# Linear attention and a gated feed-forward on one core: last stores on SyncE, batch 2's loads held by batch 1's q, and a new written order

## Chip, core and metric

The kernel runs on one core of a Trainium2 chip. The metric is the device time of the program in microseconds (us), lower is better. The core's engines are named as the profile names them: PE (TensorE; PEld is its weight load), DVE (VectorE), ACT (ScalarE), POOL (GpSimd), SP (SyncE). SP, ACT and POOL issue DMAs; the rows SPq, ACTq and POOLq are their sequencers.

## What is computed

Inputs q, k, v are 8 batches x 8 heads x 576 positions x 64, in float32. The attention is linear, with the feature map phi, and its output, laid out as 4608 tokens x 512, goes through a product of two projections and two more matrices:

```python
phi(x) = where(x > 0, x, exp(x) - 1) + 1
kv  = einsum('bhsd,bhse->bhde', phi(k), v);  z = sum(phi(k), axis=2)
num = einsum('bhsd,bhde->bhse', phi(q), kv)
den = einsum('bhsd,bhd->bhs', phi(q), z)[..., None] + 1e-06
x   = (num / den), heads side by side          # 4608 x 512
out = (((x @ w1) * (x @ w2)) @ w3) @ w_out     # w1, w2: 512 x 1024; w3: 1024 x 1024; w_out: 1024 x 512
```

## The kernel before

**Tiling.** 576 positions are 4 x 128 and 64 left over. For each batch the first 512 are one chunk (0 to 7). The 64 left of two batches are put together as a "pair" on 128 partitions; the four pairs make chunk 8. All matmuls are in bfloat16, with sums in float32. Since nothing stands between w3 and w_out, the kernel first multiplies them into one 1024 x 512 matrix (`wf_sb`).

**Steps.** Each piece of work is a small function registered under a short name (`@step`, lines 92 to 449), and the whole program is a list of such steps with arguments, the string `ORDER` (line 451 on). Each engine does its own instructions strictly in that order; semaphores between the engines are set where data or buffers require them. Nothing else decides the order, so "a new order" means a new string. The steps that matter here, with b for the batch, c for the chunk, p for the pair:

- `const:i`: memsets; `const:1` makes the 128 x 128 identity on POOL. `warm:n,i`: n matmuls on zeros, whose result nobody reads. `zr` clears half of a pair's phi(k) tile.
- Loads: `ld:k,b,h0,nh,queue` (L119) loads heads of k, q or v of a batch, 1 MB for 8 heads; `lr` (L127) the left-over 64 positions of one batch, `lp` (L135) those of a pair in two DMAs, 128 KB each; `l3` (L159) a row block of w3, `lo` (L151) of w_out, `lw` (L144) columns of w1 or w2. The last letter is the issuing queue: g POOL, s SP, a ACT. Full loads share 5 buffers (`ld`, with w3's rows among them).
- phi: `x` (exp on ACT, L166), `t` (max and add on DVE, L172), `m` (min on DVE, L180); `xr`, `tr`, `mr` the same for a pair. `v` and `vr` (L217, L225) cast v to bfloat16; a last letter a or v here means ACT or DVE.
- Attention: `kv:b,hp` (L238, L241) is phi(k)^T v with z for two heads, into PSUM; `kc` and `kh` (L248, L259) copy it out; `qt` and `qc` (L267, L273) transpose phi(q) on PE for batches 0 and 1, `qd` and `qdr` (L279, L285) by a DMA transpose on SP for the others; `na` (L291) multiplies, `nd` (L297 to L299) divides on DVE, three instructions; `nar`, `ndr` for pairs. `xp` and `xc` (L333, L338) transpose x on PE for batches 0 to 2, `xd` and `xdr` (L343, L348) on SP.
- Weights: `w3t`, `w3c` transpose w3's rows on PE and copy them; `wa`, `wf` (L373, L381) form the product w3 w_out, and `wc` copies it.
- Feed-forward: `f:c,f` (L393) is one 128-column block of x w1 and x w2 (8 matmuls of 512 columns), `fk` a part of one; `ac` (L407) copies the first on ACT and `ab` (L412) multiplies on DVE. `o:c,m` (L418) is the last product for 128 tokens (8 matmuls), `oc` (L424) its copy to SBUF and `st` (L436) its store: one DMA of 256 KB, for chunk 8 two of 128 KB. `ol:7,3` (L445 to L449) is o, oc and st of one unit in two column halves: the first is copied by DVE and stored by SP, the second by ACT both.

PSUM has four single banks for `f`, `o`, `xp`, `w3t` and warm, and two double ones for `kv`, `na` and `wa`.

**Gates.** `GATES` (line 523) names steps that must wait for another one's DMA to land although no data ties them. Before, they are two: `ld:q,2` waits for `ld:q,1`, and `lr:k,1` for `lw:0,0`. A held DMA holds all that stands behind it on its queue.

**Order around the change.** POOL makes the identity, then issues w3's and w_out's rows, batch 0, the rest of the weights and batch 1, and after that all stores but ol's. SP issues the left-over loads and all loads from batch 2 on, in the order `lr:k,1 lr:v,1 lp:v,1 ld:v,2 lp:k,1 ld:k,2 ld:q,2 ld:v,3 ...`, and the transposes between them. Batch b + 1's attention is woven between the f and o units of chunk b. At the end PE does `f:8,1 ol:7,3 o:6,0 o:6,3 f:8,2 f:8,4 o:6,2 o:8,3 o:8,1 o:8,0 o:8,2 o:7,0`.

Of the kernel before, what the change touches and what calls it, by code (L numbers as in the profile page):

```python
# [9 lines left out]
BF16 = mybir.dt.bfloat16  # L10
# [3 lines left out]
P = 128  # L14
# [4 lines left out]
def kernel(  # L19
# [12 lines left out]
    B, H, S, D = q.shape  # L32
# [51 lines left out]
    def got(d, key, pool, shape, dtype, tag, name=None):  # L84
        if key not in d:
            d[key] = pool.tile(shape, dtype, tag=tag, name=name or tag)
        return d[key]
# [114 lines left out]

    @step
    def zr(p, w):
        d = ph["kr", p, w] = phr_p.tile([P, H * D], BF16, tag="kr", name="kr")
        nc.vector.memset(d[rows_of(1 - w)], 0.0)

    @step
# [240 lines left out]
                queue.dma_start(out=dst[:, cols], in_=d[r, cols])  # L449
# [12 lines left out]
    ld:k,1,0,8,g kh:0,3,1,a kh:0,3,0,a na:0,1 na:0,0 qc:0,2,2,a w3t:6 nd:0,1 ld:q,1,0,8,g w3t:7 w3c:6,a
    nd:0,0 na:0,3 xp:0,1 w3c:7,a nd:0,3 ld:v,1,0,4,g lr:k,1,s na:0,2 xp:0,0 wf:6 lr:v,1,s nd:0,2
    xc:0,1,a xc:0,0,a ld:v,1,4,4,g fk:0,0,0,2 wc:6,v xp:0,2 xp:0,3 xc:0,2,a xc:0,3,v fk:0,0,2,1
    fk:0,0,3,1 ac:0,0,a ab:0,0 f:0,2 ac:0,2,a f:0,3 xr:k,0,1 tr:k,0,1 ab:0,2 ac:0,3,a mr:k,0,1 wf:7
    ab:0,3 f:0,5 wc:7,a vr:1,v ac:0,5,a f:0,7 ab:0,5 x:k,1,0,4 t:k,1,0,4 t:k,1,4,4 f:0,6 ac:0,7,a
    m:k,1,0,1 x:k,1,4,4 ab:0,7 m:k,1,0,0 ac:0,6,a m:k,1,4,2 f:0,4 m:k,1,4,3 x:q,1,4,4 lp:v,1,s t:q,1,0,4
    ab:0,6 ac:0,4,a ld:v,2,0,8,s f:0,1 x:q,1,0,4 t:q,1,4,4 ab:0,4 v:1,0,4,a m:q,1,0,1 m:q,1,4,2
    v:1,6,2,a m:q,1,4,3 kv:1,0 m:q,1,0,0 kv:1,1 ac:0,1,a lp:k,1,s kv:1,3 v:1,4,2,v kc:1,0,1,1,a qt:1,2,2
    kc:1,0,1,0,v kh:1,3,1,a kh:1,3,0,v ab:0,1 qt:1,0,2 qc:1,2,2,a kv:1,2 qc:1,0,2,v o:0,0 kh:1,2,0,a  # L470
    ld:k,2,0,8,s kh:1,2,1,a na:1,2 oc:0,0,a na:1,0 o:0,2 nd:1,2 st:0,0,g ld:q,2,0,8,s v:2,4,4,a vr:2,v
    nd:1,0 vr:3,a xp:1,2 na:1,1 oc:0,2,v v:2,0,4,a xp:1,0 na:1,3 nd:1,1 o:0,1 st:0,2,g xc:1,0,a
    ld:v,3,0,8,s nd:1,3 xc:1,2,a xp:1,1 oc:0,1,v xp:1,3 o:0,3 xc:1,1,a tr:k,1,2 st:0,1,g xr:k,1,2
# [24 lines left out]
    ac:4,1,a f:4,2 ld:v,7,0,8,s ab:4,1 ac:4,2,a f:4,5 ab:4,2 x:q,6,4,4 t:q,6,4,4 t:q,6,0,4 x:q,6,0,4
    f:3,1 m:q,6,4,2 m:q,6,4,3 ac:4,5,a m:q,6,0,0 m:q,6,0,1 ac:3,1,a ab:4,5 o:4,0 qd:6 x:k,6,4,4 ab:3,1
    t:k,6,0,4 x:k,6,0,4 o:4,3 t:k,6,4,4 oc:4,0,a tr:q,0,2 xr:q,0,2 m:k,6,4,2 st:4,0,g m:k,6,4,3  # L500
    ld:k,7,0,8,s m:k,6,0,1 kv:6,2 oc:4,3,v o:4,2 mr:q,0,2 st:4,3,g m:k,6,0,0 kv:6,0 oc:4,2,v kv:6,1
    qdr:0 kv:6,3 v:7,0,4,a o:4,1 st:4,2,g kc:6,0,2,1,v v:7,4,4,v kc:6,0,2,0,v na:5,1 oc:4,1,v f:3,5
    nd:5,1 st:4,1,g ac:3,5,a xd:5 na:6,0 na:6,3 ab:3,5 o:3,1 nd:6,3 nd:6,0 o:3,3 oc:3,1,v x:k,7,0,4
    t:k,7,4,4 st:3,1,g ld:q,7,0,8,s x:k,7,4,4 t:k,7,0,4 o:3,0 m:k,7,0,1 oc:3,3,a m:k,7,0,0 m:k,7,4,2
    st:3,3,g m:k,7,4,3 kv:7,0 oc:3,0,a kv:7,2 kv:7,3 st:3,0,g kv:7,1 o:3,2 kc:7,0,2,1,v kc:7,0,2,0,v
    na:6,2 oc:3,2,v na:6,1 f:5,7 nd:6,1 st:3,2,g nd:6,2 ac:5,7,a f:5,6 xd:6 ab:5,7 ac:5,6,a nar:0 nar:1
    ab:5,6 f:5,3 x:q,7,4,4 t:q,7,4,4 lp:q,1,s x:q,7,0,4 ndr:1 f:5,2 m:q,7,4,3 ac:5,3,a m:q,7,4,2 ab:5,3
    ac:5,2,a t:q,7,0,4 f:5,4 m:q,7,0,0 ab:5,2 ac:5,4,a m:q,7,0,1 ndr:0 qd:7 f:6,1 ab:5,4 ac:6,1,a f:6,7
    xdr:0 ab:6,1 ac:6,7,a lp:q,2,s f:6,4 ab:6,7 lp:q,3,s ac:6,4,a f:6,2 ab:6,4 ac:6,2,a na:7,3 na:7,2
    ab:6,2 f:6,6 nd:7,2 xr:q,1,2 tr:q,1,2 ac:6,6,a mr:q,1,2 f:6,5 nd:7,3 qdr:1 ab:6,6 ac:6,5,a na:7,0  # L510
    f:5,1 ab:6,5 nd:7,0 ac:5,1,a f:6,0 ab:5,1 ac:6,0,a f:5,0 ab:6,0 xr:q,2,2 tr:q,2,2 ac:5,0,a mr:q,2,2
    na:7,1 qdr:2 f:5,5 ab:5,0 xr:q,3,2 tr:q,3,2 nd:7,1 ac:5,5,a nar:2 mr:q,3,2 xd:7 nar:3 ab:5,5 o:5,1
    ndr:2 ndr:3 o:5,0 qdr:3 oc:5,1,a st:5,1,g xdr:1 o:5,2 oc:5,0,a st:5,0,g o:5,3 oc:5,2,a st:5,2,g
    f:7,0 oc:5,3,a st:5,3,g ac:7,0,a nar:4 f:7,6 ab:7,0 ndr:4 ac:7,6,a nar:5 f:7,3 ab:7,6 ndr:5 ac:7,3,a
    xdr:2 nar:7 f:7,1 ab:7,3 ac:7,1,a ndr:7 f:7,4 ab:7,1 ac:7,4,a f:7,7 ab:7,4 ac:7,7,a nar:6 f:7,5
    ab:7,7 ndr:6 ac:7,5,a xdr:3 f:7,2 ab:7,5 ac:7,2,a f:6,3 ab:7,2 ac:6,3,a o:7,1 ab:6,3 o:7,2 oc:7,1,a
    st:7,1,g o:6,1 oc:7,2,a st:7,2,g f:8,5 oc:6,1,a st:6,1,g ac:8,5,a f:8,0 ab:8,5 ac:8,0,a f:8,3 ab:8,0
    ac:8,3,a f:8,6 ab:8,3 ac:8,6,a f:8,7 ab:8,6 ac:8,7,a f:8,1 ab:8,7 ac:8,1,a ol:7,3 ab:8,1 o:6,0 o:6,3
    oc:6,0,a st:6,0,g f:8,2 oc:6,3,a st:6,3,g ac:8,2,a f:8,4 ab:8,2 ac:8,4,a o:6,2 ab:8,4 o:8,3 oc:6,2,v
    st:6,2,g o:8,1 oc:8,3,a st:8,3,g o:8,0 oc:8,1,a st:8,1,g o:8,2 oc:8,0,v st:8,0,g o:7,0 oc:8,2,v  # L520
    st:8,2,g oc:7,0,a st:7,0,g
    """
    GATES = "ld:q,2,0,8,s<ld:q,1,0,8,g lr:k,1,s<lw:0,0,256"
    ctx.enter_context(tc.manual_schedule())
    gates = dict(g.split("<") for g in GATES.split())

# [36 lines left out]
```

## Time and profile before

| | |
|---|---|
| median of 3 runs | 253.93 us (253.4 to 255.26) |
| profiled execution, its own time | 255.21 us |
| its span, first to last instruction | 253.5 us |
| mean granted PE clock | 0.987 |
| bytes moved | 50.06 MB, mean 198 GB/s |
| PE / DVE / ACT / POOL busy | 237.5 / 163.9 / 122.4 / 43.9 us |

A profile is one execution. Times in it count from the span's start. In a timeline row the first number is the start, the second the duration, then engine, line, operation, output<-inputs, shape and count; in square brackets stands how long the engine sat idle before it, and who ended that. In the chain of waits a row is a piece of the path that ended last; "issue" is time for which no wait is shown. The view of stretches gives for each the busy time and count of PE, PEld, DVE, ACT and POOL, then the granted clock, the DMA engines' share and GB/s. Ends of matmuls are modelled; starts are measured. Of a DMA the row on its queue is the issue alone; the landing is told separately.

### The profile page before, as it was taken

The numbers are of one execution on the slowest core, as the hardware profiler recorded it, in microseconds if no ns is written. First come the engines' busy times: TensorE is split into PE (matmuls) and PEld (weight loads), VectorE is DVE, ScalarE is ACT, GpSimd is POOL, SyncE is SP. The second block draws the span as 40 slices with busy tenths as digits, with TensorE's granted clock in tenths as the row PEclk, the third lists the DMA queues.
The fourth block names the chain that finished last, engine by engine and source line by source line (L and its number), as shares of the span: only waits on it lengthen the run. The fifth ranks groups of instructions, "written<-read, shape, count | busy, mean of one in ns | idle before, by whom it ended". The sixth has DMA issues, their size and how long they took to land.

```text
span 253.5 us, 4049 instructions
## 1 busy us (share of the span) xinstructions
PE 237.5 (94%) x1482; PEld 126.1 (50%) x1498; DVE 163.9 (65%) x364; ACT 122.4 (48%) x190; POOL 43.9 (17%) x74
## 2 busy tenths in 40 slices
PE   4997889979999999999999999999999999999991
PEld 4843854445544554554544454544544544445440
DVE  7407774877878999959557989786873564141320
ACT  3408554876857774666654814263442323322210
POOL 8544820001100210021000022100002000200133
PEclk9799999999999999999999999999999999999997
DMA  6999999999999998999999599866319311301154
GB/s 116 199 266 349 212 198 306 299 231 307 318 252 254 319 281 228 242 247 324 212 275 348 133 287 203 304 127 125 82 21 188 106 21 21 127 0 51 73 124 124
DMA packets 68915, 50.06 MB, mean 198 GB/s; under 512 B 41312, under 2 KB 64096, under 8 KB 68896
## 3 DMA queue, kind: packets, MB, share of 16 engines
q1 hardware_dynamic: 58768, 28.97, 49.0%
q0 software_dynamic: 9984, 20.71, 31.4%
q8 instruction: 11, 0.18, 0.3%
q10 hardware_dynamic: 144, 0.13, 0.2%
q14 instruction: 8, 0.07, 0.1%
HBM read 38.80 MB, written 9.44 MB: 190 GB/s over the span
## 4 chain that ended last, share of the span: by engine, by line
PE 69%; DMA 19%; DVE 5%; issue 2%; POOL 2%; ACT 1%; POOLq 0%; ACTq 0%
PE b_ps L393 22%; PE a_ps L393 22%; PE o_ps L418 19%; DMA v<-in_v_dram 8%; DMA q<-in_q_dram 5%; DMA w_sb<-in_moe_w_dram 4%; DMA wo<-in_moe_w_out_dram 3%; PE kvp L238 2%; DVE xn L299 2%; PE nd L291 2%; POOL w3b L159 1%; PE ndr L316 1%; POOL out_dram L436 1%; PE o_ps L445 1%; DVE r L298 1%
## 5 line engine op out<-in xcount | busy, mean ns | idle before, releaser
L393 PEld LDWEIGHTS <-w_sb 128*128 128x128 bf16 x576 | 55.5, 98 | 63.9 <-issue 0.6
L412 DVE TENSOR_TENSOR ab<-a_sb,b_ps 128x512 bf16<-128x512 f32 x72 | 48.9, 684 | 44.1 <-PE b_ps L393 40.8
L407 ACT COPY a_sb<-a_ps 128x512 f32<-128x512 f32 x72 | 42.0, 584 | 60.4 <-PE a_ps L393 55.7
L393 PE MATMUL a_ps<-xt,w_sb 128*128 128x512 bf16 x256 | 66.0, 379 | 0.4 <-ACT xt L338 0.4
L393 PE MATMUL b_ps<-xt,w_sb 128*128 128x512 bf16 x256 | 66.0, 379 | 0.0
L418 PE MATMUL o_ps<-wf_sb,ab 128*128 128x512 bf16 x267 | 62.7, 379 | 0.7 <-DVE ab L412 0.2
L436 POOL DMA_DIRECT2D out_dram<-o_sb x39 | 22.1, 567 | 193.5 <-ACT o_sb L424 167.8
L418 PEld LDWEIGHTS <-ab 128*128 128x128 bf16 x280 | 26.6, 98 | 29.0 <-DVE ab L412 0.3
L424 ACT COPY o_sb<-o_ps 128x512 f32<-128x512 f32 x24 | 14.0, 584 | 33.7 <-PE o_ps L418 31.3
L299 DVE TENSOR_TENSOR xn<-nd,r 128x512 bf16<-128x512 f32 x32 | 22.1, 691 | 1.1
L166 ACT ACTIVATE e<-q 128x1024 bf16<-128x1024 f32 x16 | 16.5, 1056 | 1.0 <-DMA q<-in_q_dram 1.0
L166 ACT ACTIVATE e<-k 128x1024 bf16<-128x1024 f32 x16 | 16.4, 1058 | 0.5 <-DMA k<-in_k_dram 0.5
L238 PE MATMUL kvp<-vt,k 128*128 128x130 bf16 x128 | 11.2, 220 | 2.0 <-ACT vt L217 1.2
L217 ACT CAST vt<-v 128x1024 bf16<-128x1024 f32 (+1 forms) x11 | 10.2, 934 | 5.6 <-PE kvp L238 3.1
L424 DVE COPY o_sb<-o_ps 128x512 f32<-128x512 f32 x11 | 7.6, 686 | 8.1 <-PE o_ps L418 8.0
L180 DVE TENSOR_TENSOR k<-t,e 128x512 bf16<-128x512 bf16 x32 | 12.2, 419 | 0.6 <-ACT e L166 0.3
L180 DVE TENSOR_TENSOR q<-t,e 128x512 bf16<-128x512 bf16 x32 | 11.9, 419 | 0.2
L238 PEld LDWEIGHTS <-k 128*128 128x128 bf16 x128 | 9.0, 97 | 5.8 <-issue 2.7
L291 PE MATMUL nd<-kvb,qt 128*128 128x130 bf16 x128 | 10.9, 220 | 1.0 <-DVE kvb L248 0.4
L172 DVE TENSOR_SCALAR t<-k 128x1024 bf16<-128x1024 f32 x16 | 10.5, 686 | 1.2 <-DMA k<-in_k_dram 1.2
L172 DVE TENSOR_SCALAR t<-q 128x1024 bf16<-128x1024 f32 x16 | 10.9, 687 | 0.4 <-DMA q<-in_q_dram 0.4
L291 PEld LDWEIGHTS <-qt 128*128 128x128 bf16 x128 | 8.7, 97 | 4.9 <-DVE xn L299 1.0
(70 smaller groups left out, 196.1 us busy)
## 6 DMA issues: line engine op xcount, KB each, us to landing
out_dram<-o_sb POOLq DMA_DIRECT2D x31, 256.0 KB, 5.4
v<-in_v_dram SPq DMA_DIRECT2D x6, 1024.0 KB, 11.9
k<-in_k_dram SPq DMA_DIRECT2D x6, 1024.0 KB, 9.0
q<-in_q_dram SPq DMA_DIRECT2D x6, 1024.0 KB, 8.9
w3b<-in_moe_w_dram POOLq DMA_DIRECT2D x8, 256.0 KB, 8.2
v<-in_v_dram POOLq DMA_DIRECT2D x3, 512.0 KB, 19.1
k32r<-in_k_dram SPq DMA_DIRECT2D x8, 128.0 KB, 10.8
v32r<-in_v_dram SPq DMA_DIRECT2D x8, 128.0 KB, 5.0
```

Of the source, the lines that this page charges most:

```text
L166: return nc.scalar.activation(out=e[:, 0:nh * W], in_=raw[n, b][:, h0 * W:(h0 + nh) * W], func=AF.Exp)
L172: nc.vector.tensor_scalar(out=d[:, 0:nh * W], in0=raw[n, b][:, h0 * W:(h0 + nh) * W], scalar1=0.0, scalar2=1.0, op0=ALU.max, op1=ALU.add)
L180: nc.vector.tensor_tensor(out=d[:, hp].rearrange("p j u d -> p u j d"), in0=ts[n, b, h0][:, s].rearrange("p (u j d) -> p u j d", u=2, j=NJ ...
L238: nc.tensor.matmul(dst, kj[:, hp, j].rearrange("p u d -> p (u d)"), vt[:, j, 2 * hp:2 * hp + 2, :].rearrange("p h e -> p (h e)"), start=(j ...
L291: nc.tensor.matmul(o[:, j // 2, (j % 2) * 256:(j % 2) * 256 + PW], sb["qt", b][:, hp, j * P:(j + 1) * P], kvb[b][:, hp].rearrange("p u e - ...
L299: nc.vector.tensor_tensor(out=dst, in0=o[:, :, :, 0:D], in1=r.unsqueeze(3).to_broadcast(list(r.shape) + [D]), op=ALU.mult)
L393: nc.tensor.matmul(o, w[:, kc, f * P:(f + 1) * P], xt_of(c)[:, :, kc, :], start=(kc == 0), stop=(kc == KC - 1))
L407: return copy_of[eng](out=d, in_=ps["a", c, f])
L412: nc.vector.tensor_mul(out=d[:, f, :], in0=sb["a", c, f], in1=ps["b", c, f])
L418: nc.tensor.matmul(d, sb["ab", c][:, f, m * P:(m + 1) * P], wf_sb[:, f, :], start=(f == 0), stop=(f == FC - 1))
L424: return copy_of[eng](out=d, in_=ps["o", c, m])
L436: queue_of[queue].dma_start(out=dst, in_=sb["o", c, m][r])
```

## The change

No function computes anything else than before, and the steps are the same but for queues and engines. What differs:

- `zr` takes its tile by `got`, so that `zr:0,0` may now stand after `mr:k,0,0` in the order.
- Two gates become six: `lp:k,1`, `ld:k,2`, `lp:v,1`, `ld:q,2` and `ld:v,2`, all of batch 2's transfers, wait for `ld:q,1` to land; `lr:k,1` waits as before.
- Stores of chunk 8 and of units 7,1, 7,2 and 7,0 are issued by SP instead of POOL; `ol:7,3` is PE's last unit.
- The order is another one throughout. SP's loads come as k, q, v of a batch, instead of v first; `const:1` follows `l3:4`; `w3t:5 w3t:4` stand before `wa:7`; `wf:7` before the first `fk`; some copies change between ACT and DVE.

```diff
     def zr(p, w):
-        d = ph["kr", p, w] = phr_p.tile([P, H * D], BF16, tag="kr", name="kr")
+        d = got(ph, ("kr", p, w), phr_p, [P, H * D], BF16, "kr")
         nc.vector.memset(d[rows_of(1 - w)], 0.0)
...
-    GATES = "ld:q,2,0,8,s<ld:q,1,0,8,g lr:k,1,s<lw:0,0,256"
+    GATES = "lp:k,1,s<ld:q,1,0,8,g ld:k,2,0,8,s<ld:q,1,0,8,g lp:v,1,s<ld:q,1,0,8,g ld:q,2,0,8,s<ld:q,1,0,8,g ld:v,2,0,8,s<ld:q,1,0,8,g lr:k,1,s<lw:0,0,256"
```

The new order in the stretches that the prediction speaks of (start; PE from the last wa to the first fk; batch 1; the transpose xd:3; the end):

```
const:0 const:2 lr:k,0,s const:9 l3:0 lr:v,0,s const:11 l3:1 warm:26,0 const:3 l3:2 l3:3 lo:0,2
xr:k,0,0 const:6 lo:2,2 const:8 const:7 lo:4,2 zr:0,1 tr:k,0,0 lo:6,2 mr:k,0,0 const:10 l3:4 const:4
const:1 l3:5 zr:0,0 const:5 w3t:0 ld:k,0,0,4,g warm:8,1 w3c:0,a w3t:1 ...
... wa:6,1 l3:6 w3t:5 w3t:4 w3c:5,a wa:7,1 l3:7 t:k,0,0,4 w3c:4,a wf:5 ...
... wf:7 nd:0,3 xc:0,1,v nd:0,2 xp:0,3 fk:0,0,0,2 wc:7,v xc:0,3,a xp:0,2 xc:0,2,v fk:0,0,2,1 fk:0,0,3,1
...
ac:0,5,a f:0,4 ab:0,5 ac:0,4,a t:k,1,0,4 x:k,1,4,4 f:0,6 t:k,1,4,4 x:k,1,0,4 ab:0,4 m:k,1,4,2
ac:0,6,a f:0,7 m:k,1,0,0 m:k,1,0,1 ab:0,6 x:q,1,0,4 lp:k,1,s t:q,1,0,4 f:0,3 ac:0,7,a m:q,1,0,0
ld:k,2,0,8,s m:q,1,0,1 v:1,0,4,a m:k,1,4,3 ab:0,7 ac:0,3,a kv:1,1 t:q,1,4,4 qt:1,0,2 x:q,1,4,4
ab:0,3 kv:1,0 o:0,2 v:1,6,2,a kc:1,0,1,1,v lp:v,1,s m:q,1,4,3 qc:1,0,2,a m:q,1,4,2 kc:1,0,1,0,a
v:1,4,2,a qt:1,2,2 oc:0,2,v na:1,1 ld:q,2,0,8,s kv:1,2 qc:1,2,2,a st:0,2,g nd:1,1 kv:1,3 o:0,3
kh:1,2,1,a kh:1,3,0,a kh:1,3,1,v kh:1,2,0,v ld:v,2,0,8,s xp:1,1 x:k,2,0,4 t:k,2,4,4 na:1,2 na:1,0
oc:0,3,v o:0,1 xr:k,1,2 nd:1,2 st:0,3,g x:k,2,4,4 ld:k,3,0,8,s nd:1,0 xc:1,1,a na:1,3 xp:1,2
oc:0,1,a m:k,2,4,3 o:0,0 nd:1,3 xc:1,2,a st:0,1,g tr:k,1,2 vr:3,a t:k,2,0,4 xp:1,3 vr:2,a xp:1,0
m:k,2,0,0 x:q,2,0,4 xc:1,3,v lp:k,2,s xc:1,0,v m:k,2,0,1 oc:0,0,a f:1,1 ...
...
v:4,4,4,a qd:4 na:3,2 f:2,2 ab:2,6 v:4,0,4,a nd:3,2 ac:2,2,a nd:3,0 f:2,1 ab:2,2 x:k,5,0,4 t:k,5,0,4
ac:2,1,a kv:4,1 t:k,5,4,4 kv:4,2 lp:v,3,s x:k,5,4,4 kv:4,0 ab:2,1 na:3,3 kv:4,3 nd:3,3 o:2,1
kc:4,0,2,1,a kc:4,0,2,0,a qdr:0 m:k,5,0,1 m:k,5,4,2 m:k,5,0,0 o:2,2 m:k,5,4,3 xr:k,3,2 xd:3 oc:2,1,v
tr:k,3,2 st:2,1,g mr:k,3,2 na:4,2 oc:2,2,v o:2,0 nd:4,2 st:2,2,g na:4,0 oc:2,0,v o:2,3 nd:4,0
st:2,0,g vr:6,a ld:q,5,0,8,s na:4,1 oc:2,3,v na:4,3 nd:4,3 st:2,3,g f:3,7 ...
...
f:8,1 ab:8,2 ac:8,1,a f:8,0 ab:8,1 ac:8,0,a f:8,4 ab:8,0 ac:8,4,a f:8,7 ab:8,4 ac:8,7,a o:6,1 ab:8,7
o:8,2 oc:6,1,a st:6,1,g o:8,3 oc:8,2,a st:8,2,s o:8,0 oc:8,3,v st:8,3,s f:7,1 oc:8,0,a st:8,0,s
ac:7,1,a o:8,1 ab:7,1 o:7,1 oc:8,1,v st:8,1,s o:7,2 oc:7,1,v st:7,1,s o:7,0 oc:7,2,a st:7,2,s ol:7,3
oc:7,0,v st:7,0,s
```

## The prediction

> **What bounds the kernel now.** I read the page first: busy times and the slices.
>
> ```profile
> span 253.5 us, 4049 instructions
> PE 237.5 (94%) x1482; PEld 126.1 (50%) x1498; DVE 163.9 (65%) x364; ACT 122.4 (48%) x190; POOL 43.9 (17%) x74
> ...
> DMA  6999999999999998999999599866319311301154
> ```
>
> PE is the bound, but "busy" takes in pipelined waiting. Start to start, a 512-column matmul takes 0.216 us in this trace; counting every matmul of the program so (a unit f or o 8 x 0.216 = 1.73, kv 0.28, na or xp 0.22, qt 0.44) gives 231.5 us, the same before and after, since the same units are only reordered. The last matmul ends at 247.8: about 16 us of PE's time is waiting, and 5.7 us follow it. The DMA row says that transfers run without a pause for the first 145 us. The windows table places the waiting:
>
> ```profile
> 38.00:51.50 13.50, 13.50 (x64) 6.14 (x63) 9.00 (x18) 9.08 (x14) 0.00 (x0) 1.00 1.10 294
> 51.50:65.60 14.10, 11.91 (x102) 7.19 (x102) 10.66 (x28) 9.97 (x18) 1.65 (x3) 1.00 1.13 291
> 65.60:150.00 84.40, 83.85 (x515) 43.33 (x518) 69.59 (x156) 52.38 (x79) 7.06 (x12) 1.00 1.02 260
> 150.00:228.60 78.60, 78.35 (x424) 38.05 (x427) 47.80 (x106) 28.79 (x47) 6.97 (x12) 1.00 0.49 117
> ```
>
> The second column is the stretch, the third PE's busy time. After 65.6 only 0.8 us is idle in 163 us. So there are three places: the start (to 38), batch 1's attention (51.5 to 65.6), and the end. PE's own timeline, and the chain of waits, for batch 1:
>
> ```profile
> 52.92 0.22 PE L241 MATMUL kvp<-vrz,kr 128*128 128x130 bf16 x1
> 54.34 0.39 PE L238 MATMUL kvp<-vt,k 128*128 128x130 bf16 x4 [1.20 <-ACT vt L217]
> ```
>
> ```profile
> 33.15 20.48 DMA v<-in_v_dram
> 53.63 0.02 issue
> 53.65 0.64 ACT vt L217
> ```
>
> Batch 1's v lands at 53.6, 20.5 us after its issue. The DMA view of 31.5 to 53.6 says who shared the engines with it:
>
> ```profile
> q0 software_dynamic: 2768, 4.63, 86.8%
> q1 hardware_dynamic: 2708, 1.13, 29.2%
> ```
>
> q1 is SP's queue: 1.13 MB, of which only 0.26 (two lr loads) is batch 1's. 0.87 MB is ld:v,2 (issued 35.7) and the pair loads of batches 2 and 3. The end, from the chain, and the two halves of unit ol from the timeline:
>
> ```profile
> 244.39 0.70 DVE o_sb L424
> 245.09 1.70 issue
> 246.79 0.46 POOL out_dram L436
> 247.25 0.07 issue
> 247.31 0.88 POOL out_dram L436 x2
> 248.20 0.15 issue
> 248.35 0.53 POOL out_dram L436
> 248.88 0.56 POOLq L558
> ```
>
> ```profile
> 230.16 0.38 SPq L449 DMA_DIRECT2D out_dram<-o_sb  x1
> ...
> 230.98 0.37 ACTq L449 DMA_DIRECT2D out_dram<-o_sb  x1
> ```
>
> PE is done at 247.8 and the last copy at 248.4, but POOL still issues stores until 249.4, five in a row at 0.53 each, after 1.7 us in which the profile shows nothing that it waited for.
>
> **What the Trainium skill says.** "DMA: Bandwidth & Descriptors", section "Issuing engines are not separate DMA queues": transfers from SP, ACT and POOL run on the same 16 engines and interleave. The trace agrees (the two queues above). So holding SP's loads leaves the engines to POOL's. The same page, "Latency and other measured facts", gives about 0.6 us to the first byte for SP's path and 1 us for POOL's; here a 128 KB store lands 2.0 us after its issue on SP and 2.5 on POOL, the same direction. "TensorE: Matmul & The Clock Gate", Part 1: after some 3.4 us of idleness PE runs at half clock, 107 ns for 128 columns against 56. The trace shows both (8 transposes 1.06 us at 9.4, 0.61 at 11.15).
>
> **The change part by part.**
>
> *Start.* POOL's first l3 starts at 0.74 where the identity's two instructions stand now, instead of 1.45: 0.7 earlier. POOL's issues are chained to landings (from the ninth on, each starts just after the landing of the one eight before), so I carry 0.6 of it to all POOL loads. The identity moves behind l3:4, ends near 7.0 by POOL's row durations, and w3t:0 goes from 6.2 to 7.0; its warm-up risk is up to 1 us. Placing w3t:4 and 5 before wa:7 removes most of the 1.7 us wait for w3t; wf:7 (1.73) moves ahead of the first f into waiting time. PE would reach batch 1's kv about 2.3 us earlier, 49.5 for 51.8. None of that is kept unless v is there.
>
> *Gates.* lp:k,1, ld:k,2, lp:v,1, ld:q,2 and ld:v,2 wait for batch 1's q: 30.7 + 18.2 = 48.9 now (the DMA issues), so 48.3. SP holds nothing else between. Until 48 the hardware queue took little besides lr, so q gains nothing but the 0.6. Then v: the software queue has 0.55 MB left at 48, which at about 310 GB/s is 1.8 us; v's halves land near 49.6 and 50.4, not 51.2 and 53.6. The second is 3.2 earlier.
>
> *Batch 1's attention.* First half's cast on ACT (1.05) behind x:q,1,0,4 and ac:0,7: done near 51.1; kv:1,1 at 51.2 for 52.4 now. ACT then has ac 0.58, x 1.06, v 0.63, qc 1.0, kc 0.26, v 0.63: 55.3, so kv:1,2 at 55.4. PE fills with o:0,2 and qt, then o:0,3 to 57.7. DVE: nd:1,1 to 56.4, two kh, t:k,2 0.69, oc 0.69, nd:1,2 and nd:1,0 (1.1 each) to 60.8, nd:1,3 to 62.1, tr, t, two xc (0.42 each): 64.1. So f:1,1 starts at 64.1, the first f of chunk 1 now at 65.7: **1.6 us gained**, DVE's chain keeping the rest. Bounds: nothing (v no earlier), 3.2 (all of v's gain).
>
> *What is late next.* Batch 2's k, issued after lp:k,1 at about 49.6, lands near 55 for 62.7 now, wanted at 56.8. q2 lands about 59, v2 62.5 (now 58.4), wanted at 64 and 67.5. By 53.6 the engines have moved the same bytes, in another order. From there k3 to k5 are wanted earlier: by PE work placed before them, 58.5 for 71.8, 74.2 for 88.7, 90.3 for 97.2; v later. Counted as the tenth load, k5 moves 6.9 us. Loads arrive barely in time now (q3 lands at 76.5, its first reader starts at 76.6). With SP's order I get k4 at 85 (wanted 87), v4 98 (99.6), k5 102 (103.3). No stall, 1 to 2 us of slack.
>
> *Transposes on SP.* xd:3 now has 12 us to f:3,7, in the new order 6.5 (four o, four na and a kv, less the wait for nd:3,3), behind qdr:0; they take 4.3 to 7.5 from issue to landing: 0 to 1 us lost, taken as zero against the 0.8 idle us after 65.6 that an order may recover. xd:7 has 7.9, transfers being thin there. Copies swapped between ACT and DVE (0.58 against 0.69) are hidden by f units there: zero; if cover were gone, 0.1 each.
>
> *End.* Stores of chunk 8 and three of chunk 7 move to SP, 7 more DMA steps (11 DMAs at 0.38, far under the 1.73 of an o). ol moves to the end at the same PE work. From ol now: PE ends 230.54, ACT's half is issued 230.98 and lands 1.9 later, 2.4 after PE. DVE copies its half to 230.13 and then oc:7,0 (0.69) to 230.85; st:7,0, 256 KB, lands about 2.3 after its issue: 2.7 after PE's end. Now it is 252.1 - 247.8 = 4.3 (last issue 248.9 plus 3.3, the longest landing among the last ten). **1.6 us gained**; bounds 1.0 and 2.2. The 1.4 us after the last landing stay.
>
> Sum: 253.5 - 1.6 - 1.6 = 250.3 for the span. The profiled execution took 255.2 (span and 1.7 around it), above the median of 253.93; applied to the median: **250.7**.
>
> **Rivals.**
> 1. *Only the end* (chance 0.20): v is ahead, but ACT and DVE, 10 and 10.7 us busy of 14.1 there, set f:1 as now. For it: their chain above already keeps half. Against: the 1.2 us wait is v's. 253.9 - 1.6 = 252.3.
> 2. *All is kept* (0.17): the full 3.2 of v, 1.6 at the end, 0.8 of later idle time and 0.4 of landing: 247.9.
> 3. *Loads become the bound* (0.18, the slow side): the hardware queue starts 0.87 MB behind and doesn't recover it, so that k5 lands where it does now (108.2) instead of at 103.3; DVE's t:k,5 stands ahead of ab:2,1 and nd:3,3, and PE waits for both. That is 4.9 us lost, 255.6; with 0.87 MB at 260 GB/s, 3.3 more: 258.9. It ends my gain when k5 lands after 106.5 and is over 1% slower after 109. Against: the same bytes by 53.6, and a gap in demand (k5 to q5) after it.
> That the gates do nothing is no rival: SP's loads issued 32.8 to 48.5 are all named.
>
> **How the numbers follow.** Forecast 0.45 (249.4 to 252.0), rivals 0.20, 0.17, 0.18. 1% is 2.5 us, about what a measurement of this kernel can tell from no change: faster below 251.4. Most of the forecast and rival 2 give 0.56; the rest of the forecast, rival 1 and a third of rival 3 are the same, 0.32; slower 0.12. Range 247.8 to 255.0, which leaves the outer part of rival 3 and a little of 2.
>
> **What would show it.** Right: v's second half lands near 50.4, kv:1 starts near 51.2, the first f of chunk 1 near 64, the last landing 2.7 after PE's end. Wrong: DVE or ACT waiting for k or q of batches 2 to 5 with PE idle behind them; f:3,7 waiting for xd:3; PE in f later than 65.7; a half-clock stretch past 12 us.

## The result and the profile after

The change moved nothing that can be measured. With 20 runs of each side by side, the kernel before took 255.03 us (253.4 to 257.91) and the changed one 255.3 us (254.17 to 256.29); the ratio is 1.0009, 95% interval 0.999 to 1.0028. The prediction was 250.7. Of the 4.6 us between, 1.1 are the first median of before, 253.93 from three runs, which more runs put at 255.03; 3.2 are the gain that was forecast and didn't come, and 0.3 lie between the two medians.

The profiled execution of the changed kernel took 255.47 us. Its page has the same span as before within 0.2 us. PE is 0.8 us busier, but 16 of its 1498 matmuls are missing from the trace of before (x1482 there), so that this difference says little:

```profile
span 253.3 us, 4047 instructions
PE 238.3 (94%) x1498; PEld 126.7 (50%) x1498; DVE 165.0 (65%) x364; ACT 125.2 (49%) x190; POOL 37.4 (15%) x63
...
DMA  6999999999999999999993999999406413000543
```

The view of stretches, with the same four stretches (stretch, its length, then PE, PEld, DVE, ACT and POOL busy):

```profile
38.00:51.50 13.50, 12.98 (x67) 6.05 (x66) 9.86 (x21) 7.15 (x11) 0.00 (x0) 1.00 1.06 297
51.50:65.60 14.10, 13.33 (x112) 7.76 (x109) 13.21 (x33) 13.00 (x22) 1.65 (x3) 1.00 1.13 295
65.60:150.00 84.40, 82.71 (x520) 43.09 (x521) 69.88 (x160) 54.40 (x81) 6.34 (x12) 1.00 1.05 255
150.00:228.60 78.60, 78.43 (x420) 37.82 (x419) 45.53 (x97) 29.29 (x48) 7.12 (x13) 1.00 0.54 121
```

Read against the lines of before, this already says where to look. From 51.5 to 65.6 PE is 1.4 us busier, but DVE is busy 13.21 of the 14.10 us (10.66 before) and ACT 13.00 (9.97 before): both helpers are now full there. From 65.6 to 150, where PE had 0.55 us of idle time, it has 1.69.

To compare kernels I count PE's waiting much as in the prediction: start to start of successive matmuls, less 0.216 us for 512 columns (in proportion for fewer), with the missing matmuls of before put in as done. The 1.2 us ahead of the first matmul are left out. The count is mine, from the trace of one execution each:

| us | waiting up to the last `fk` | from there to the first `f` of chunk 1 | after that | PE's end | last landing after it |
|---|---|---|---|---|---|
| before | 10.4 | 2.9 | 1.1 | 247.8 | 4.3 |
| after | 12.1 | 1.6 | 2.0 | 249.1 | 2.8 |

So the two gains that were meant are there: 1.3 us less waiting up to chunk 1's first `f` and 1.5 us less at the end. They are paid back with 1.7 us up to the last `fk` and 0.9 us after chunk 1's first `f`.

*The start.* PE's waits by releaser (total us, times, longest), of before and then of after, and the first transposes in the timeline, in the same order:

```profile
PE w3p L356 <- DMA w3b<-in_moe_w_dram: 2.5, 2, 2.1
PE wf_ps L381 <- DVE w3t L365: 1.7, 1, 1.7
...
PE w3p L356 <- POOL ident masks.py:199: 3.4, 1, 3.4
PE kvp L238 <- DVE kvb L248: 1.8, 1, 1.8
PE a_ps L393 <- DVE xt L338: 1.8, 2, 1.3
```

```profile
6.20 0.62 PE L356 MATMUL w3p<-ident,w3b 128*128 128x128 bf16 x8 [2.05 <-DMA w3b<-in_moe_w_dram]
...
1.26 2.29 POOL L159 DMA_DIRECT2D w3b<-in_moe_w_dram  x4 [0.81 <-POOLq L547]
...
7.20 0.29 POOL masks.py:199 TENSOR_SCALAR_AFFINE_SELECT ident<-ident 128x128 bf16<-128x128 bf16 x1
7.54 1.01 PE L356 MATMUL w3p<-ident,w3b 128*128 128x128 bf16 x8 [3.39 <-POOL ident masks.py:199]
```

PE waits 3.4 us for the identity and starts w3's transposes at 7.5, where it started at 6.2 before. What was to pay for this didn't: the first load of w3 is issued at 1.26 instead of 1.45, 0.2 us earlier and not 0.7, since POOL is idle until 1.26 even with nothing ahead of the load. The 1.7 us wait for the copy of w3t is 0.2 now, as predicted, but a wait of 1.8 us for the copy of kv has come up behind it. One sign that the prediction named, a half-clock stretch past 12 us, came too, if barely. Groups of 8 transposes or warm matmuls take 0.95 to 1.06 us up to the one that starts at 11.76, and 0.61 from 12.54 on. Six groups are slow; before there were four, in a stretch for which that trace shows a granted clock of 0.50 (8 to 10 us). The changed kernel's trace has no clock entry before 12.4 us.

*Batch 1.* v's halves land at 49.8 and 52.1 (51.1 and 53.6 before). Its casts and what follows:

```profile
52.29 1.06 ACT L217 CAST vt<-v 128x1024 bf16<-128x1024 f32 x1
53.72 0.39 PE L238 MATMUL kvp<-vt,k 128*128 128x130 bf16 x4
...
64.22 0.69 DVE L172 TENSOR_SCALAR t<-k 128x1024 bf16<-128x1024 f32 x1
65.29 0.75 DVE L338 COPY xt<-xtp 128x512 bf16<-128x512 bf16 x2
66.09 1.04 PE L393 MATMUL a_ps<-xt,w_sb 128*128 128x512 bf16 x4 [1.26 <-DVE xt L338]
```

The first half has been there for 2.5 us when ACT casts it, so the data no longer bind here. Nor does the cast, which ends at 53.35: PE comes straight from chunk 0's last `f` and isn't free sooner. At the far end `f:1,1` waits for two copies of transposed x, which stand on DVE behind phi of batch 2's k. Before, the first `f` of chunk 1 (`f:1,7` in that order) starts 0.4 us earlier:

```profile
65.66 1.03 PE L393 MATMUL a_ps<-xt,w_sb 128*128 128x512 bf16 x4
```

*The end.* PE's end in the timeline:

```profile
248.73 0.33 SPq L449 DMA_DIRECT2D out_dram<-o_sb  x1
249.15 0.37 ACT L447 COPY o_sb<-o_ps 128x256 f32<-128x256 f32 x1 [2.84 <-PE o_ps L445]
249.33 0.33 SPq L436 DMA_DIRECT2D out_dram<-o_sb  x1
249.55 0.37 ACTq L449 DMA_DIRECT2D out_dram<-o_sb  x1
```

PE ends at 249.1, the last issue is at 249.55, the last landing at 251.95.

### The profile page after: what moved, and what is told of

Same layout as the page of the kernel before. It is cut to its first block, busy times and chain, and to the rows that moved or that the text cites. A ratio compares the mean times of both kernels' runs of the same rounds, so it can differ in the third digit from the quotient of the medians.

```text
span 253.3 us, 4047 instructions
## 1 busy us (share of the span) xinstructions
PE 238.3 (94%) x1498; PEld 126.7 (50%) x1498; DVE 165.0 (65%) x364; ACT 125.2 (49%) x190; POOL 37.4 (15%) x63
## 4 chain that ended last, share of the span: by engine, by line
PE 71%; DVE 16%; ACT 5%; issue 4%; POOL 2%; DVEq 0%; ACTq 0%; POOLq 0%
PE a_ps L393 20%; PE b_ps L393 20%; PE o_ps L418 19%; DVE xn L299 3%; PE wa L373 3%; ACT e L166 2%; PE kvp L238 2%; DVE t L172 2%; DVE ab L412 2%; PE w3p L356 2%; DVE k L180 1%; DVE r L298 1%; DVE q L180 1%; PE nd L291 1%; PE warm L113 1%
## 5 line engine op out<-in xcount | busy, mean ns | idle before, releaser
L418 PE MATMUL o_ps<-wf_sb,ab 128*128 128x512 bf16 x280 | 64.9, 379 | 0.1
L436 POOL DMA_DIRECT2D out_dram<-o_sb x28 | 15.7, 559 | 186.2 <-ACT o_sb L424 105.1
L418 PEld LDWEIGHTS <-ab 128*128 128x128 bf16 x280 | 26.6, 98 | 29.6 <-DVE ab L412 0.9
L424 ACT COPY o_sb<-o_ps 128x512 f32<-128x512 f32 x18 | 10.5, 584 | 27.6 <-PE o_ps L418 27.6
L424 DVE COPY o_sb<-o_ps 128x512 f32<-128x512 f32 x17 | 11.7, 688 | 11.2 <-PE o_ps L418 11.2
L172 DVE TENSOR_SCALAR t<-k 128x1024 bf16<-128x1024 f32 x16 | 10.7, 689 | 8.6 <-DMA k<-in_k_dram 8.6
L217 ACT CAST vt<-v 128x1024 bf16<-128x1024 f32 (+1 forms) x15 | 14.3, 970 | 0.0
L180 DVE TENSOR_TENSOR k<-t,e 128x512 bf16<-128x512 bf16 x32 | 12.1, 421 | 2.8 <-ACT e L166 2.4
L172 DVE TENSOR_SCALAR t<-q 128x1024 bf16<-128x1024 f32 x16 | 10.7, 687 | 0.4 <-DMA q<-in_q_dram 0.4
```

Source lines behind the costliest of these rows:

```text
L172: nc.vector.tensor_scalar(out=d[:, 0:nh * W], in0=raw[n, b][:, h0 * W:(h0 + nh) * W], scalar1=0.0, scalar2=1.0, op0=ALU.max, op1=ALU.add)
L180: nc.vector.tensor_tensor(out=d[:, hp].rearrange("p j u d -> p u j d"), in0=ts[n, b, h0][:, s].rearrange("p (u j d) -> p u j d", u=2, j=NJ ...
L418: nc.tensor.matmul(d, sb["ab", c][:, f, m * P:(m + 1) * P], wf_sb[:, f, :], start=(f == 0), stop=(f == FC - 1))
L424: return copy_of[eng](out=d, in_=ps["o", c, m])
L436: queue_of[queue].dma_start(out=dst, in_=sb["o", c, m][r])
```

## The experiments

All were timed in five rounds beside the kernel before; ratios are to it, with a 95% interval. 1% is 2.55 us.

**1. The parts alone.** The end on before's order, and the gates on before's order:

```diff
 # e1: before, with the end
-ol:7,3 ab:8,1 ... st:8,3,g ... st:8,1,g ... st:8,0,g ... oc:7,0,a st:7,0,g
+ab:8,1 ... st:8,3,s ... st:8,1,s ... st:8,0,s ... st:8,2,s ol:7,3 oc:7,0,v st:7,0,s
 # e2: before, with the six gates (arguments shortened)
-GATES = "ld:q,2<ld:q,1 lr:k,1<lw:0,0"
+GATES = "lp:k,1<ld:q,1 ld:k,2<ld:q,1 lp:v,1<ld:q,1 ld:q,2<ld:q,1 ld:v,2<ld:q,1 lr:k,1<lw:0,0"
```

> The kernel before with the end of the change alone: chunk 8's stores and st:7,0 on SP, ol:7,3 as the last unit, oc:7,0 on DVE. Theory (the end is worth what the trace of the changed kernel shows: last landing 2.5 us after PE's end instead of 4.3): 1.7 us less, ratio 0.993, PE's end unchanged at 247.8. Rival (the end's gain is given back after the landing, in the closing steps on POOL and SP): ratio 0.998 or more.

> The kernel before with the change's six gates alone. Theory (the gates are what ended PE's waits in batch 1's attention): v's second half lands near 51.5 instead of 53.6, PE's 1.4 us wait at 52.9 goes, 1.0 to 1.5 us less, ratio 0.995. Rival (in this order v of batch 2 goes first and is cast at 58.7, just after it lands; held until 49 it lands later and DVE or ACT wait for it): the gain is eaten or reversed, ratio 0.999 to 1.006.

The end alone: 0.9936 (0.9913 to 0.996), 1.6 us, with the last landing 2.9 us after PE's end. The gates alone: 0.998 (0.9956 to 1.0004), some 0.5 us and not resolved from nothing. In e2's trace v lands at 49.9 and 51.7, and `f:1,7` starts at 63.8. That is not all the gates' doing: in e1's trace, without them, v lands at 50.0 and 52.4 and `f:1,7` starts at 64.5, both earlier than in the trace of before.

**2. Is it SP or the unit placed last?** e8 leaves `ol:7,3` where before has it and only moves chunk 8's stores and `st:7,0` to SP.

> The kernel before with chunk 8's stores and st:7,0 on SP, ol:7,3 left where it was. Theory (the queue is the whole gain of the end: POOL's five stores at 0.53 each and its 1.7 us pause go, and a full unit last costs the same as two halves): last landing 2.9 after PE's end, ratio 0.994 as e1. Rival (the halves matter): landing 3.5 after PE's end, ratio 0.9965.

0.993 (0.9911 to 0.9949), the same as e1. The queue is the whole gain as far as these intervals tell (0.2% each way); the unit in two halves at the very end adds nothing that shows.

**3. Both parts on before's order.** e7 is e1 with e2's gates.

> The kernel before with the end of e1 and the gates of e2 and its own order. Theory (the two parts add, and the new order is what loses them): 1.6 plus 0.5, ratio 0.991 to 0.992. Rival (they share a limit): ratio 0.9936 as e1.

0.9906 (0.9872 to 0.9941), 2.4 us faster than before. By these figures the end and the gates add up, though the intervals of e1 and e7 overlap. The third part of the change, the new order, costs 1.0009 - 0.9906 = 1.03%, or 2.6 us: all that the other two bring. Here the intervals don't overlap.

**4. Undoing single steps of the new order.** e3 puts the identity back ahead of the first load of w3; e4 gives the changed kernel before's two gates; e5 is e3 with batch 5's k later on DVE and ACT; e6 is e5 with one exp of batch 0 earlier.

```diff
 # e3: after, identity first
+const:1 l3:0 ... l3:4 const:4
-l3:4 const:4 const:1
 # e5: e3, with
-ab:2,2 x:k,5,0,4 t:k,5,0,4 ac:2,1,a kv:4,1 t:k,5,4,4 ... ab:2,1 na:3,3 kv:4,3 nd:3,3
+ab:2,2 ac:2,1,a x:k,5,0,4 kv:4,1 ... ab:2,1 na:3,3 kv:4,3 nd:3,3 t:k,5,0,4 t:k,5,4,4
 # e6: e5, with
+x:k,0,4,4 x:q,0,0,4
-x:k,0,4,4 lw:1,1,256
```

> The changed kernel with const:1 (the identity) put back ahead of the first l3 on POOL; nothing else. Theory (the start loses 1.5 us because PE waits 3.4 us for the identity, and ACT's copies, exp of k and kv:0,2 follow from that): first w3t near 6.2 instead of 7.5, first f near 37.6 instead of 39.0, 1.3 us less than the changed kernel, ratio to before 0.995 to 0.997. Rival (the start is set by ACT's own order of copies and exponentials, or by the loads): first f stays within 0.4 us of 39.0, ratio to before 1.000.

> The changed kernel with the two gates of before. Theory (in the new order PE reaches batch 1's kv at 53.7, later than v lands even without gates, so the gates buy nothing here): batch 1's kv:1,2 and the first f of chunk 1 within 0.5 us of 57.3 and 66.1, ratio to before 0.999 to 1.003. Rival (the gates are what removed 1.5 us of waits): first f of chunk 1 at 67.5 or later, ratio 1.006.

> The changed kernel with the identity first (as e3), and the first readers of batch 5's k moved behind chunk 2's last ab: x:k,5,0,4 behind ac:2,1, both t:k,5 behind nd:3,3. Theory (the time won at the start in e3 was lost again at 106, where DVE and ACT stand waiting for batch 5's k ahead of the copy and the product that PE's next o needs): the 1.2 us wait at 106.4 is gone, first f of chunk 3 near 114.2 instead of 115.3, 1.0 us less than e3, ratio to before 0.997. Rival (another load or a transpose is as late, and the wait moves on): the sum of PE's waits after the first f of chunk 1 stays near 3 us, ratio 1.001.

> As e5, and x:k,0,4,4 ahead of x:q,0,0,4 on ACT, where the kernel before has it. Theory (the new order's start is slow because exp of the second half of batch 0's k comes third, and DVE waits 0.9 us for it ahead of kc and kv:0,2): the wait before kv:0,2 falls from 1.3 to under 0.6 us, first f of chunk 0 about 0.8 us earlier than e5, ratio to before 0.994. Rival (the start is set by v's landing at 26.4 and the chain of small copies after it): first f within 0.3 us of e5's, ratio 0.997.

e4: 1.0036 (1.0017 to 1.0055). That is 0.7 us above the changed kernel (1.0036 less 1.0009), but the intervals overlap. Where the gates were meant to help they do nothing in this order: e4's v lands at 52.4 and 54.1, 2.6 and 1.9 us later than in the changed kernel, and PE starts batch 1's kv and chunk 1's first `f` no later (53.6 and 66.0, for 53.7 and 66.1). From e4's timeline:

```profile
53.60 0.39 PE L238 MATMUL kvp<-vt,k 128*128 128x130 bf16 x4
...
65.98 1.04 PE L393 MATMUL a_ps<-xt,w_sb 128*128 128x512 bf16 x4 [1.26 <-DVE xt L338]
```

The two traces part later, at 108.7, where batch 5's k landed at 106.2 (105.1 in the changed kernel) and PE waits 0.9 us (0.2). The other three came out level: e3 1.0012 (0.9989 to 1.0035), e5 1.0007 (0.9988 to 1.0027), e6 0.9997 (0.998 to 1.0015). In e6 the first `f` starts 0.1 us earlier than in e5, where 0.8 was expected.

e3 is the instructive one. The wait for the identity is gone, w3's transposes start at 6.2 again and `f:1,1` starts 1.1 us earlier than in the changed kernel (65.0 for 66.1), yet `f:3,7` starts at 115.3 for 115.5. The microsecond is lost on the way. The timeline of e3:

```profile
105.31 1.29 DVE L172 TENSOR_SCALAR t<-k 128x1024 bf16<-128x1024 f32 x2 [0.30 <-DMA k<-in_k_dram]
...
107.85 3.19 PE L418 MATMUL o_ps<-wf_sb,ab 128*128 128x512 bf16 x14 [1.04 <-DVE r L297]
```

DVE stands before batch 5's k, which has only just landed, and behind it wait the last product of chunk 2 and the division of batch 3, for which PE stops 1.04 us. In the changed kernel DVE comes to this place at 106.0, after the landing (105.1), and PE waits 0.2 us. e5 takes this wait away, and PE waits 0.8 us seven microseconds later, for a division of batch 4 on the same DVE. Time gained before 100 us is taken back here in large part: of the 1.1 us by which e3 leads the changed kernel at `f:1,1`, 0.2 are left at `f:3,7`; of e5's 1.3, 0.8.

**5. Where in the new order?** e9 is before's sequence up to the first `fk` and the new one after it; e10 is the new one up to there and before's after it. Both have the end and the gates.

> The changed kernel with the start of its order (all steps up to the first f, weights included) in the sequence of the kernel before, and the new order from there. Theory (the new order loses in two places, 1.5 us or more at the start and 1.1 after the first f of chunk 1): PE's waits before the first f fall by 1.2 us or more against e3, first f of chunk 1 near 64, but part is lost again where the new order waits for batch 5's k near 105; ratio to before 0.995 to 0.999. Rival (the start of both orders is worth the same once the identity is first): as e3, ratio 1.000 to 1.002.

> The complement: the new order's steps up to the first f, then the order of the kernel before, with the change's end and gates (e7 with the new start). Theory: PE starts batch 1 about 1.5 us later than in e7, waits after the first f of chunk 1 stay near 0.9 us as before, ratio 0.996 to 0.998. Rival (the late start is made up, since v of batch 1 sets when its attention can go on): ratio 0.991 as e7.

| | before's order from the first `fk` | new order from there |
|---|---|---|
| before's start | e7: 0.9906 (0.9872 to 0.9941) | e9: 0.9991 (0.9966 to 1.0016) |
| new start | e10: 0.9934 (0.9912 to 0.9955) | after: 1.0009 (0.999 to 1.0028) |

Down a column the start makes 0.2 to 0.3%, less than these intervals resolve. Along a row the rest of the order makes 0.75 to 0.85%, about 2 us. So the start, where PE's waiting had shown the largest single loss, is the smaller part, and what comes after it is the larger one. The traces say the same in another way. Between the first `f` of chunk 1 and PE's end both orders do the same work; it takes 182.1 us in five of the seven traces with before's order there (before, e1, e2, e7, e10; e8 183.5, e11 183.0) and 183.0 to 184.1 in all eight with the new one. PE's waits of over 0.3 us after 60 us, with the place, are in e9: 1.43 (62.7), 0.74 (87.6), 0.46 (105.6), 0.72 (136.8), 0.33 (189.2); in e7: 0.35 (60.9) and 0.38 (89.9).

**6. Are these waits the loss?** e15 covers four of the five in e9.

```diff
 # e15: e9, with
-tr:k,1,2 t:k,2,0,4 m:k,2,0,0 ... xc:1,3,v xc:1,0,v
+xc:1,3,v xc:1,0,v tr:k,1,2 t:k,2,0,4 m:k,2,0,0
-xp:2,0 xp:2,2 xc:2,3,a kv:3,3
+xp:2,0 kv:3,3 xp:2,2 xc:2,3,a
-x:k,5,0,4 t:k,5,0,4 ac:2,1,a kv:4,1 t:k,5,4,4 ... ab:2,1
+ac:2,1,a x:k,5,0,4 kv:4,1 ... ab:2,1 t:k,5,0,4 t:k,5,4,4
-na:5,1 f:4,7
+f:4,7 na:5,1
```

> The version with before's start and the changed order after it (0.9991 of before), with the four waits of PE after 60 us covered: DVE does the two xc of batch 1 ahead of tr:k,1,2, t:k,2,0,4 and one m (wait 1.26 us, worth some 0.7, since the copies themselves stay); kv:3,3 stands between xp:2,0 and xp:2,2 (wait 0.58, worth 0.3); ac:2,1 and ab:2,1 go ahead of the exp and max of batch 5's k, which lands late (wait 0.3); f:4,7 stands ahead of na:5,1 (wait 0.55). Theory A (the loss of the changed order is these waits): 1.85 us less, 0.9991 - 0.0073 = 0.992, about 252.0 us beside before at 254.1. Rival (covering a wait on DVE or ACT moves it to the next one, as with batch 5's k alone): 0.997 to 1.000, and the trace shows PE waiting in new places after 60 us.

0.9981 (0.9959 to 1.0004): of the 0.73% hoped for, 0.1% came back, less than the interval resolves. The waits did shrink, to 0.79, 0.45, nothing and 0.4 us (and one of 0.41 came up at 70). But PE now stops at the first `f` of chunk 3 (waits by releaser, and the timeline):

```profile
PE a_ps L393 <- DMA xt<-xn: 0.8, 1, 0.8
...
PE a_ps L393 <- DVE xt L338: 0.6, 1, 0.6
```

```profile
110.12 1.89 SPq L343 DMA_TRANSPOSE xt<-xn  x1
...
116.19 1.02 PE L393 MATMUL a_ps<-xt,w_sb 128*128 128x512 bf16 x4 [0.85 <-DMA xt<-xn]
```

The transposed x of chunk 3 (`xd:3`) is issued at 110.1 and lands at 116.15. In the kernel before it is issued at 102.6, lands at 110.0 and is wanted at 114.9; in the changed one it is issued at 109.0, lands at 115.0 and is wanted at 115.5. It hangs on `nd:3,3`, the division that stands behind batch 5's k. With half a microsecond of slack it is a floor for what is gained ahead of it. In e3, e6, e9 and e15 `f:3,7` starts 0.04 us after the landing (115.3, 114.8, 114.1 and 116.2). As these times show, the floor moves with `nd:3,3`: e9 leads the changed kernel by 1.9 us at `f:1,1` and still by 1.4 at `f:3,7`.

**7. The floor moved.** e17 is e15 with `xd:3` earlier:

```diff
-kv:4,1 ... ab:2,1 t:k,5,0,4 t:k,5,4,4 na:3,3 kv:4,3 nd:3,3 ... qdr:0 ... xd:3
+na:3,3 kv:4,1 ... ab:2,1 nd:3,3 t:k,5,0,4 t:k,5,4,4 kv:4,3 ... xd:3 qdr:0
-oc:2,1,v oc:2,2,v oc:2,0,v oc:2,3,v
+oc:2,1,a oc:2,2,a oc:2,0,a oc:2,3,a
```

> The version with the four waits covered (0.9981), and chunk 3's last division earlier: na:3,3 ahead of kv:4,1, nd:3,3 straight behind ab:2,1, xd:3 ahead of qdr:0 on SP, and the four oc of chunk 2 back on ACT, as before the change, so that DVE has 2.7 us less between 107 and 117 us. Theory (xd:3 is the floor at 115 us): it lands two or more us earlier, PE's wait of 1.0 us there and that of na at 114.5 go, 0.9981 - 0.0055 = 0.993, about 252.2 us beside before at 254.1. Rival (there is always a next wait, here k and q of batch 5 or nd on DVE): 0.997 to 1.0 with a new wait of about 1 us between 107 and 130 us.

0.9964 (0.9945 to 0.9984). Of the 0.55% hoped for, 0.17% came, with overlapping intervals. `xd:3` lands at 112.1, PE's wait for it is gone and `f:3,7` starts at 113.3. Of these 2.9 us against e15's trace, 2.2 stand already at the first `fk`, where both have the same code (34.8 and 37.0; see the last section); 0.7 are the edit's. The next wait stands already, 0.65 us at 94.7, and has the same form (timeline of e17):

```profile
93.67 1.30 DVE L172 TENSOR_SCALAR t<-q 128x1024 bf16<-128x1024 f32 x2 [1.45 <-DMA q<-in_q_dram]
94.88 0.68 DVE L412 TENSOR_TENSOR ab<-a_sb,b_ps 128x512 bf16<-128x512 f32 x1
95.61 1.02 PE L393 MATMUL b_ps<-xt,w_sb 128*128 128x512 bf16 x4 [0.49 <-DVE ab L412]
```

Batch 4's q has only just landed; DVE waits for it with `ab` behind it, and PE's `f` behind that.

**8. A splice at chunk 3.** e14 is e7 up to the first `f` of chunk 3 and the new order from there; e16 is the same with two pair loads issued ahead of batch 5's k.

> Before's order up to the first f of chunk 3, the changed order from there, with the end on SP and the six gates in both parts. The version with before's order all through stood at 0.9906 of before, the one with the changed order after the first f of chunk 0 at 0.9991, 2.1 us more. Theory A (the loss is the waits of PE that the trace shows): of the changed order's waits, the one before the first f of chunk 1, the one at 89 and the one at 107 us go; those of na at 138 (0.72 us) and 191 (0.33 us) stay, so 0.9906 + 1.05/254 = 0.995, about 252.8 us beside before at 254.1. Theory B (all of the loss is the loads' and DVE's crowding up to 107 us): 0.990 to 0.992. Theory C (the later part of the order costs in a way that no wait of PE shows, such as denser weight loads or slower matmuls): 0.997 or more.

> Before's order to the first f of chunk 3 and the changed one from there, with the end and the gates, and with lp:q,0 and lp:v,3 now issued ahead of batch 5's k, so that nothing at the joint waits for them. Theory A (the loss is what PE's waits show): only the waits of na near 138 and 191 us remain, 1.05 us, so 0.9906 + 0.0041 = 0.995. Theory B (all is lost before 107 us): 0.990 to 0.992. Theory C (the later part costs in a way that no wait shows): 0.997 or more. A new wait at the joint of over 0.5 us makes it undecided; its size is then told from the trace.

1.0406 (1.0367 to 1.0444) and 1.0281 (1.0237 to 1.0325), and neither tells the theories apart: both have a wait at the joint that neither order has. In e14 ACT waits 10.7 us for a pair load, with PE's `f` behind it; in e16 `xd:3` is issued at 104.6 and lands 12.7 us later, at 117.3, and PE waits 3.6 us for it. In both traces the granted PE clock is 0.50 around this wait, from 119.4 to 129.6 us in e14 and from 116.5 to 123.3 in e16, whose `f` matmuls start 0.43 us apart there. The waits of `na` that e9 has at 137 and 189 are in both, at the same size (0.72 or 0.73, and 0.33), so these two do belong to the later part of the new order. What it costs by itself was not got from this pair.

**9. The gate's other half.** The gate on `lp` ties only the second of its two DMAs: the first of `lp:k,1` is issued at 32.1 in the changed kernel and the second at 48.2, when q has landed, with `ld:k,2` behind it at 48.9. e11 is e7 with both held.

```diff
-            made = queue_of[queue].dma_start(
+            made.append(queue_of[queue].dma_start(
...
+            for one in made if isinstance(made, list) else [made]:
```

> As e7, with both DMAs of each lp held; the gate of the change holds only the second of the two, and the first pair DMA of 128 KB leaves at 32. Theory (what shares the engines with batch 1's v delays it): v's second half 0.3 to 0.5 us earlier, ratio 0.989 to 0.991. Rival (with the gates on, v is no longer what PE waits for): v earlier and the time unchanged, ratio 0.991.

0.9904 (0.987 to 0.9939), no different from e7; its median of 252.44 us is the lowest of all. This version, before's order with the end and the gates, is faster than both kernels.

## Why the prediction was wrong, step by step

- **The end: right.** 1.6 us were predicted, 1.6 came (e1). The last landing was put at 2.7 us after PE's end and was at 2.84. What the prediction didn't separate is that SP alone does it (e8). Two things shrink in the traces. From PE's end to the last issue it was 1.06 us, and is 0.44 in e1 and 0.65 in e8. The last store then took 3.26 us to land, and takes 2.44 and 2.34. The Trainium skill, "DMA: Bandwidth & Descriptors", section "Latency and other measured facts", gives SP's path about 0.4 us less to the first byte than POOL's; the 0.8 to 0.9 us of the landing are twice that. POOL's five last stores landed after 2.28, 2.67, 2.46, 3.07 and 3.26 us, so that the row itself may slow its end; this was not shown.
- **The gates: v came earlier, by less than put, and it bought little.** v's first half was put at 49.6 and landed at 49.8; the second at 50.4 and landed at 52.1. The term that failed is POOL's 0.55 MB "at about 310 GB/s" after q. The gates end with q's landing, not v's, and from then on SP's held loads run beside v. The DMA view of 48.2 to 52.1 in the changed kernel:

```profile
q1 hardware_dynamic: 945, 0.48, 60.7%
q0 software_dynamic: 130, 0.44, 36.3%
```

SP's queue (q1) moved more than POOL's (q0), which got 0.44 MB in 3.9 us. On before's order the gates brought 0.5 us (e2, not resolved from nothing), in the new order nothing at batch 1 (e4).
- **"PE would reach batch 1's kv about 2.3 us earlier": this step failed.** PE came to it at 53.7, 1.3 us later than before (52.4). Three terms of the step were off. The loads are chained as the prediction read it (from POOL's ninth on, 16 of 21 are issued 0.28 to 0.33 us after the landing of the one eight before), but their head hardly moved: the first load by 0.2 us, and with the identity put back ahead of it (e3) v lands at 49.9 and 52.2, within 0.1 us of the changed kernel. The identity was ready at 7.5, 0.5 us later than put. And the wait that left w3t came back as a wait for kv's copies. `wf:7` did go ahead of the first `fk`, but into no waiting time, since that time is filled by instructions that wait one after another.
- **"f:1,1 starts at 64.1": wrong through the step before.** It started at 66.1, 2.0 us late, and PE was 2.5 us late at kv already (53.7 for 51.2). From kv to `f:1,1` the prediction had 12.9 us and the trace has 12.4. It is 12.4 in all six traces that have the new order in this stretch as it stands (after, e3, e4, e5, e6, e9), with the gates and without them (e4). In e9, where PE comes to kv at 51.8, `f:1,1` starts at 64.2. So rival 1's doubt, that ACT and DVE and not v set this stretch, was right for the new order; with two copies ahead of phi of k on DVE it falls to 11.7 (e15, e17).
- **"No stall, 1 to 2 us of slack" and xd:3 "taken as zero": the slack wasn't there, though it cost the changed kernel little.** Batch 5's k was put at 102 and landed at 105.1, 1.8 us after the 103.3 at which it was wanted. DVE came to it at 106.0, PE waited 0.2 us, and `xd:3` landed 0.6 us before its reader. Rival 3 named the place (DVE's phi of k,5 ahead of `ab:2,1` and `nd:3,3`) and put the harm too high, at 4.9 us. It shows in the variants: PE waits 1.0 us there in e3, which comes early, and 0.9 in e4, which doesn't, but whose k lands 1.1 us later.
- **The new order as a sum of zeros: this step failed, and by the runs it is the larger.** The prediction costed the swap of work between 66 and 228 us at nothing, because before had 0.8 us of idle time there to win. It could also lose, and it did: 0.75 to 0.85%, about 2 us, by the table of e7, e9, e10 and after, batch 1's part included. In the changed kernel's trace PE waits 0.74 us at 90.3, 0.72 at 139.0 and 0.33 at 191.0, each time for a division on DVE; the largest such wait of before after chunk 1's first `f` is 0.38.

In the two profiled executions the forecast of 3.2 us thus came as 1.5 at the end, less 0.4 at chunk 1's first `f` and 0.9 after it: 0.2 us.

Shown: the end's share and SP as its cause; that end and gates together make before's order faster (e7); that the new order after the first `fk` takes it back. Seen in one trace each: that e15 waits for `xd:3` and e17 doesn't. Not settled: how the 2 us divide. By the traces of e7 and e9, 0.5 lie between batch 1's kv and chunk 1's first `f` (12.4 for 11.9) and 1.3 after it (183.5 for 182.1). Covering the waits brought back 0.7 us of 2.2 at most (e9 against e17, with intervals that overlap), and each cover laid bare another wait. The new order changes the loads' sequence (k, q, v) and the engines' work at once, and no run parts the two; whether a further round would reach e7 wasn't tried either. The start's own share, 0.2 to 0.3%, is within the intervals.

## What to carry to other kernels

In a hand-written order, a gain at one place can be lost at the next point that is tied to something other than that gain: a load, or a transpose hanging on one. List those points with their slack before adding up gains, and count what goes beyond the least slack as doubtful. When a change brings a queue, a few waits and a whole new order together, time the small parts on the old order first: here they were the better kernel. Elementwise work of the next batch that stands ahead of this batch's copies on DVE or ACT turns a late load into a wait of PE, even though PE reads none of that data.

## What was not expected of the hardware

- POOL issues its first DMA at 1.26 us with nothing of the kernel's own before it, against 1.45 with the identity's two instructions before it: taking away what stood from 0.74 to 1.31 moved it 0.2 us.
- The same code started differently from profile to profile: with before's start, PE reached batch 0's kv at 26.6 to 27.4 in nine traces, but at 29.0 in e15 and 29.3 in e7. Those two are the ones whose granted clock drops just ahead of it, as the view of stretches shows (PE alone; before, then e7):

```profile
24.00:26.00 2.00, 2.00 (x21) 1.00 1.05 324
...
24.00:26.00 2.00, 2.00 (x6) 0.50 1.03 342
```

At that clock e7's matmuls of 512 columns start 0.43 us apart there, for 0.216. A stretch of PE's waiting up to there is known to about 2 us from one profile, which is why the ratios, and not the counts, decide above.
- One and the same transpose, `xd:3`, took from 4.3 us (e5) over 7.5 (before) to 12.7 (e16) from issue to landing. In e16 two loads of 1 MB were issued behind it, at 111.2 and 111.8; whether they are the cause wasn't tried.
- With q of batch 1 landed, each load of 1 MB landed 4.1 to 9.3 us after the one before it in the changed kernel (k2 at 56.7, q2 61.0, v2 65.2, k3 71.1, q3 75.7, v3 82.3, k4 86.9, q4 91.6, v4 101.0, k5 105.1): the order of the loads moves who is late, not how much is moved.
